# Another order in the opening of a state-space and feed-forward kernel: one chunk's C by heads, scores ahead of a mask difference, a held weight load, transposes behind the mixes

## The chip, the core and the metric

The kernel runs on one core of a Trainium2 chip. The metric is the device time in microseconds of one execution; the time before is the median of three runs. Engines are named as the profile names them: PE is TensorE, PEld its weight loads, DVE VectorE, ACT ScalarE, POOL GpSimd, SP SyncE. SP's and ACT's sequencers also issue the DMA transfers ("SPq", "ACTq" in the profile). All times inside an execution are counted from the start of the span.

## The reference

Two blocks in a row. The first is a state-space scan over 4 batches, 8 heads and 768 steps, with head width 32 and state width 16, in float32. In short:

```python
log_a = np.log(np.clip(a, 1e-06, 1.0))
for each chunk:                       # xc, Bc, Cc, la: the chunk's slices
    cum = np.cumsum(la, axis=-1)
    L = np.exp(cum[..., :, None] - cum[..., None, :]) * causal
    M = np.einsum('bhin,bhjn->bhij', Cc, Bc) * L
    y = np.einsum('bhij,bhjd->bhid', M, xc)
    y += np.einsum('bhin,bhnd->bhid', Cc, state) * np.exp(cum)[..., None]
    state = decay_full * state + sum over j of (Bc * xc * decay_from_j)
```

The second takes y as 3072 tokens of width 256: `h = y @ w_in` (256 x 2048), `g = h * clip(h + 3, 0, 6) / 6`, `out = g @ w_out` (2048 x 256). The two weight matrices are float64 in memory.

## The kernel before

The 768 steps are handled as six chunks of 128 (index `c`), each in two halves of 64 steps. For each chunk the kernel makes masks, scores, mixes and the new state, and from the chunk's y the feed-forward block `h`, `g` and `out`, which has most of the work. All instructions are written out in one order; every engine, and each queue of DMA issues, works through its own instructions in that order and waits by semaphores. Nothing is rescheduled. A wait thus holds up everything behind it on its engine. DMA semaphores are eight, shared in turn: a transfer that takes a semaphore again first waits until the transfer that had it before has landed.

The opening is the part up to the first `h` of chunk 0. Its steps, with the lines of the profile:

- ACT issues the first quarter of w_in (`load_w(0)`, L139, 1 MB into the tile `raw`) and then B (L94). SP issues `a` (L81), then chunk 0's C in eight transfers of 32 KB (`pairs_first`, L101, tile `pairs`: one for each batch and each parity of the head), then x (`load_x`, L119, tile `xt`), then the second quarter of w_in (`load_w(1)`, L139).
- From `a`, ACT and DVE make logarithms and running sums (L264, L266, L269), for the first two chunks first. PE turns these into differences in PSUM: a constant mask (L336, L343), then `diff`, which is `diff_less` (L348) and 16 small products `diff_pick` (L357) for each batch. ACT's exponentials make the decay tiles `L` of them (L365). Chunk 0's differences lie in banks f0 to f3, chunk 1's batches 0 and 1 in the banks "o", its batches 2 and 3 in the banks y0 and y1.
- PE transposes B (L422), ACT copies the result (L431, `bT`). DVE transposes C in squares (`turn_squares`, L465, `csT`) and makes two masked copies (`part_heads`, L475, `cT`). POOL fades half of csT (`fade`, L481) and scales B (`ends`, L396). DVE sums the remaining chunks' logarithms (`add_up`, L269) and SP stores them (`store_rows`, L286, L288).
- `busy` (L493) makes products with the identity whose result nobody reads: two ahead of the scores, one ahead of the mixes. Each is two MATMUL records of PE.
- `scores` (L530, tile `cb`) multiplies C and B into banks f0 to f3, and then `into_state` (L544) makes the parts of the new state in the banks y0 and y1. `multiply` has ACT copy these (L560, L569) and DVE multiply `L` by the scores in four instructions (L574).
- `turn_cum` (L316) transposes the running sums on PE into bank f1, and `by_token` (L319, DVE) stores them negated, for later chunks' masks.
- `mix` (L604) multiplies the masked scores and x, each half of the heads followed by the products with the mid-chunk state (`from_state`, L503). `keep` (L618, ACT) copies y for the feed-forward block.
- `renew` (L587, L554, DVE) makes the new state.

The float64 weights are decoded by hand, in five steps of a generator (`decode`; `weights(i, n)` runs n steps of part i): ACT extracts the top 16 bits (L198); DVE isolates exponent and sign (L215, L217) and makes the significand in two long operations (L201, L205); ACT builds the scale in two passes (L221, L223); DVE joins sign and scale (L228) and multiplies (L236) into `w_in` or `w_out`. Three `raw` buffers are used in turn.

After the opening, `mlp_in` (L626) makes `h` for 16 column blocks f of chunk 0 in the banks f0 to f3 in turn, each from two products that PE runs as four MATMUL records; ACT makes the ramp (L730) and DVE the product with it (L735, tile `gT`), which frees the bank. Block f uses weight part f // 4. The decoding of weight parts 2 to 5 is woven in between by f. Then come the output products `first_out` (L748), which need `gT` and the decoded `w_out`.

The order around the change is these lines of the kernel body:

```python
    turn_squares(bcs[0][0], turned(0)[2])      # L998
    part_heads(0)
    fade(0, HALF[1], nc.gpsimd)
    add_up(ends_at[1])
    store_rows()
    load_w(2)
    weights(0, 1)
    busy(2, ...)
    scores(0)
    multiply(0)
    load_w(3)
    turn_cum(c_ps)                             # L1010
    busy(1, ...)
    ...
    mix(0)                                     # L1015
```

Of the kernel before, what the change touches and what calls it, by code (L numbers as in the profile page):

```python
# [8 lines left out]
FP32 = mybir.dt.float32  # L9
# [12 lines left out]
def kernel(  # L22
# [24 lines left out]
    nc = tc.nc  # L47
    P = 128
# [37 lines left out]
    def load_bc(c):  # L86

        sl = slice(c * P, (c + 1) * P)  # L90

        def tokens_first(src, queue=nc.sync, **where):
            t = loads.tile([P, NB * NH, N], FP32, **where)
            queue.dma_start(out=t, in_=src[:, :, sl, :].rearrange("b h s n -> s (b h) n"))  # L94
            return t

        def pairs_first(src):
            t = loads.tile([P, 2, NB, 4, N], FP32, name="pairs", tag="bc")
            for b in range(NB):
                for h in range(2):  # L100
                    nc.sync.dma_start(  # L101
                        out=t[:, h, b].rearrange("s a n -> s (a n)"),
                        in_=src[b, h:NH:2, sl, :].rearrange("h (s a) n -> h s (a n)", a=4))
            return t

        if 0 < c < TURN:
            bcs[c] = [tokens_first(C, name="C", tag="bc")]
        Bs[c] = tokens_first(B, nc.scalar if c == 0 else nc.sync, name="B", bufs=1)
        if c == 0:
            bcs[c] = [pairs_first(C), Bs[c]]  # L110
        elif c < TURN:
            bcs[c].append(Bs[c])
        else:
            bcs[c] = [pairs_first(C), pairs_first(B)]
# [10 lines left out]
    NRAW = 3  # L125
    raws = {}

    def load_w(i, queue=nc.sync):

        raw = loads.tile([P, NK * FP * 2 * P], U32, name="raw", bufs=NRAW)  # L130
        if i < NP:
            cols = slice(2 * i * FP * P, 2 * (i + 1) * FP * P)
            src = moe_w_in[:, cols].rearrange("(k p) f -> p k f", p=P)
            dst = raw.rearrange("p (k f) -> p k f", k=NK)
        else:
            r0 = (i - NP) * FP * P
            src = moe_w_out[r0:r0 + FP * P, :].rearrange("(k p) m -> p k m", p=P)
            dst = raw.rearrange("p (k m) -> p k m", k=FP)
        queue.dma_start(out=dst, in_=src)  # L139
        raws[i] = raw  # L140
# [1 line left out]
    load_w(0, nc.scalar)  # L142
    load_bc(0)
    load_x(0)
    load_w(1)
    nc.scalar.preload_act_table_set("natural_log_exp_and_others")


# [38 lines left out]
    def decode(i):  # L187
# [20 lines left out]
            yield  # L208

        parts_m = significand()  # L210
        if i == 0:
            next(parts_m)
            next(parts_m)
        yield
# [70 lines left out]
    def store_rows():  # L285
        nc.sync.dma_start(  # L286
            out=cum_e[1:].rearrange("c g p -> g c p"), in_=cum_c[:, 1:])
        nc.sync.dma_start(  # L288
            out=cum_d[2:].rearrange("c a g i -> g (c a) i"),
            in_=cum[:, 2 * P:].rearrange("g (k i) -> g k i", i=HT))  # L290
# [178 lines left out]
    def part_heads(c):  # L469
        _, cT, csT = turned(c)  # L470
        for t in range(2):
            if c == TURN:
                nc.scalar.activation(cT[:, :, t], csT, AF.Copy, scale=parity[:, t:t + 1])
            else:
                nc.vector.tensor_scalar(  # L475
                    out=cT[:, :, t], in0=csT, scalar1=parity[:, t:t + 1], scalar2=None,
                    op0=ALU.mult)

    def fade(c, sl=slice(0, P), engine=nc.vector):
        csT = turned(c)[2][:, :, sl]  # L480
        engine.tensor_tensor(out=csT, in0=csT, in1=etos[c][:, :, sl], op=ALU.mult)  # L481
# [8 lines left out]
    def busy(n, bank):  # L490

        for _ in range(n):
            nc.tensor.matmul(  # L493
                out=bank.rearrange("p (b i) -> p b i", b=NB), lhsT=ident,
                rhs=ident.unsqueeze(1).to_broadcast([P, NB, P]), start=True, stop=True)
# [117 lines left out]
    def keep(c):  # L613

        yTs[c] = att.tile([P, NK, NB, P], FP32, name="yT", bufs=1)
        for a, u in ((0, 0), (0, 1), (1, 0), (1, 1)) if c else ((0, 0), (1, 0), (0, 1), (1, 1)):
            y, dst = ys[c][a, u], yTs[c][:, u, :, HALF[a]]
            nc.scalar.copy(out=dst, in_=y)  # L618
# [344 lines left out]
    def weights(i, n):  # L963
        for _ in range(n):
            next(parts[i], None)


    def diff(c, *bs):
        for part in (diff_less, diff_pick):
            for b in bs:  # L970
                part(c, b)
# [19 lines left out]
    for b in range(NB):  # L991
        ends(0, b)
    turn_b(0)
    diff(1, 0, 1)
    weights(0, 1)
    diff_exp(1, 2)
    diff_exp(1, 3)
    turn_squares(bcs[0][0], turned(0)[2])  # L998
    part_heads(0)
    fade(0, HALF[1], nc.gpsimd)  # L1000
    add_up(ends_at[1])
    store_rows()
    load_w(2)
    weights(0, 1)
    busy(2, ps.tile([P, NB * P], FP32, name="d", tag="f3"))
    scores(0)
    multiply(0)
    load_w(3)
    c_ps = ps.tile([P, NC, G], FP32, name="c_ps", tag="f1")
    turn_cum(c_ps)  # L1010
    busy(1, ps.tile([P, NB * P], FP32, name="d", tag="f0"))
    weights(0, 1)
    weights(1, 1)
    by_token(c_ps)
    mix(0)  # L1015
    keep(0)
    weights(1, 3)
    renew(0)
    weights(1, 1)
    load_eto(1)  # L1020
# [155 lines left out]
```

## Time and profile before

| what | value |
|---|---|
| time, median of 3 runs | 344.33 us (343.4 to 345.18) |
| profiled execution: its time | 343.4 us |
| profiled execution: its span | 341.7 us, granted clock 1.0 |
| PE busy | 333.8 us (98%) |
| DVE busy | 210.7 us (62%) |
| ACT busy | 188.3 us (55%) |
| POOL busy | 145.4 us (43%) |
| first score product (L530) | 15.20 us |
| first `h` product (L626) | 22.54 us |
| first output product (L748) | 50.11 us |

The span is the time from the first to the last instruction of the program; the execution's time has some 1.7 us more. The shares are averages over stages with different limits: in the opening PE waits for other engines and for DMA, from the first `h` product on it runs without a break. In lines of the chain of waits the numbers are the start, the length and what ran or was waited for; in lines of a timeline they are the start, the time from the first to the last of a merged group, the engine, the line, the operation, the tiles and, in brackets, the idle time before it with what ended it. The trace also holds a record of each DMA packet (queue, start, length, size) and of each increment of a DMA semaphore; from these come the times of packets and landings.

### The profile page before, as it was taken

The numbers are of one execution on the slowest core, as the hardware profiler recorded it, in microseconds if no ns is written. First come the engines' busy times: TensorE is split into PE (matmuls) and PEld (weight loads), VectorE is DVE, ScalarE is ACT, GpSimd is POOL, SyncE is SP. The second block draws the span as 40 slices with busy tenths as digits, with TensorE's granted clock in tenths as the row PEclk, the third lists the DMA queues.
The fourth block names the chain that finished last, engine by engine and source line by source line (L and its number), as shares of the span: only waits on it lengthen the run. The fifth ranks groups of instructions, "written<-read, shape, count | busy, mean of one in ns | idle before, by whom it ended". The sixth has DMA issues, their size and how long they took to land.

```text
span 341.7 us, 8203 instructions
## 1 busy us (share of the span) xinstructions
PE 333.8 (98%) x3372; PEld 267.5 (78%) x3372; DVE 210.7 (62%) x332; ACT 188.3 (55%) x394; POOL 145.4 (43%) x139
## 2 busy tenths in 40 slices
PE   5999999999999999999999999999999999999996
PEld 2554448888878888888888888888888888888996
DVE  6699999996499739665519465528465323465011
ACT  4778878667987481675471676470576030576000
POOL 3300000381282998099803089810089600079600
PEclk9999999999999999999999999999999999999999
DMA  8989967052690216167107294001260001110000
GB/s 172 174 312 197 209 233 153 2 59 69 164 114 8 58 55 119 25 84 70 24 27 144 33 96 62 16 2 18 33 75 2 2 4 17 30 17 2 0 33 31
DMA packets 89605, 25.15 MB, mean 74 GB/s; under 512 B 82208, under 2 KB 85952, under 8 KB 89056
## 3 DMA queue, kind: packets, MB, share of 16 engines
q1 hardware_dynamic: 85184, 23.33, 36.5%
q10 hardware_dynamic: 4384, 1.31, 1.8%
q8 instruction: 26, 0.43, 0.5%
q14 instruction: 11, 0.09, 0.1%
HBM read 21.33 MB, written 3.29 MB: 72 GB/s over the span
## 4 chain that ended last, share of the span: by engine, by line
PE 94%; DMA 3%; DVE 1%; SPq 1%; issue 0%; DVEq 0%
PE h L692 33%; PE wb L874 13%; PE wc L874 8%; PE o L748 8%; PE h L626 8%; PE wa L874 8%; PE oa L810 4%; PE ob L810 4%; PE y L604 3%; PE y L503 2%; PE cb L530 2%; DMA raw<-in_moe_w_in_dram 2%; PE y L544 1%; DMA pairs<-in_C_dram 1%; SPq L101 1%; DVE L L574 0%
## 5 line engine op out<-in xcount | busy, mean ns | idle before, releaser
L735 DVE SCALAR_TENSOR_TENSOR gT<-gT,h 128x512 f32<-128x512 f32 x96 | 64.9, 686 | 41.1 <-ACT gT L730 39.9
L730 ACT ACTIVATE gT<-h,half 128x512 f32<-128x512 f32 x96 | 65.2, 684 | 17.8 <-PE h L692 15.9
L796 POOL TENSOR_TENSOR s<-gT 128x512 f32<-128x512 f32 x20 | 28.9, 1443 | 76.2 <-DVE gT L735 76.1
L711 ACT ACTIVATE h<-h 128x512 f32<-128x512 f32 x62 | 35.8, 583 | 43.6 <-PE h L692 39.3
L692 PE MATMUL h<-y_hi,w_part 128*128 128x512 f32 x160 | 51.8, 409 | 0.0
L692 PE MATMUL h<-y_less,w_part 128*128 128x512 f32 x160 | 49.7, 397 | 0.0
L692 PE MATMUL h<-y_lo,w_part 128*128 128x512 f32 x160 | 49.5, 395 | 0.0
L692 PEld LDWEIGHTS h<-y_lo,w_part 128*128 128x128 f32 x160 | 30.0, 188 | 7.4
L692 PEld LDWEIGHTS h<-y_less,w_part 128*128 128x128 f32 x160 | 30.0, 188 | 6.9
L692 PEld LDWEIGHTS h<-y_hi,w_part 128*128 128x128 f32 x160 | 30.0, 188 | 6.8 <-DVE gT L735 0.4
L385 ACT ACTIVATE L<-L,cum_n 128x64 f32<-128x64 f32 x128 | 31.6, 338 | 0.0
L874 PE MATMUL wb<-s,w_out 128*128 128x256 f32 x128 | 30.6, 382 | 0.0
L748 PE MATMUL o<-w_out,gT 128*128 128x256 f32 x128 | 28.8, 381 | 0.0
L626 PE MATMUL h<-yT,w_in 128*128 128x512 f32 x64 | 27.7, 594 | 0.0
L748 PEld LDWEIGHTS o<-w_out,gT 128*128 128x128 f32 x128 | 24.1, 190 | 3.8 <-issue 0.5
L403 POOL TENSOR_TENSOR tmp<-state,eto 128x256 f32<-128x256 f32 x5 | 3.4, 673 | 55.3 <-ACT eto L389 55.2
L874 PEld LDWEIGHTS wb<-s,w_out 128*128 128x128 f32 x128 | 24.0, 190 | 3.6
L796 POOL TENSOR_TENSOR s<-gT,s 128x512 f32<-128x512 f32 x20 | 26.0, 1306 | 1.3
L796 POOL TENSOR_TENSOR gT<-gT 128x512 f32<-128x512 f32 x20 | 25.7, 1291 | 1.3
L796 POOL TENSOR_TENSOR s<-s,gT 128x512 f32<-128x512 f32 x20 | 25.7, 1290 | 0.0
L158 POOL TENSOR_SCALAR_AFFINE_SELECT L<-L 64x1024 f32<-64x1024 f32 (+1 forms) x16 | 20.4, 1280 | 10.5 <-DMA L<-cum_d 10.1
L396 POOL TENSOR_TENSOR bs<-B,L 128x128 f32<-128x128 f32 x24 | 12.7, 545 | 26.0 <-ACT L L385 20.9
(138 smaller groups left out, 507.5 us busy)
## 6 DMA issues: line engine op xcount, KB each, us to landing
raw<-in_moe_w_out_dram SPq DMA_DIRECT2D x4, 1024.0 KB
L<-cum_d SPq DMA_DIRECT2D x8, 512.0 KB
xt<-in_x_dram SPq DMA_DIRECT2D x6, 512.0 KB
raw<-in_moe_w_in_dram SPq DMA_DIRECT2D x3, 1024.0 KB
out_dram<-back SPq DMA_DIRECT2D x128, 16.0 KB
pairs<-in_C_dram SPq DMA_DIRECT2D x40, 32.0 KB
eto<-cum_e SPq DMA_DIRECT2D x20, 64.0 KB
B<-in_B_dram SPq DMA_DIRECT2D x5, 256.0 KB
```

The source lines that it names most:

```text
L158: nc.gpsimd.affine_select(out=t[rows], in_=t[rows], pattern=pattern, compare_op=ALU.is_ge, fill=-1e5, base=base, channel_multiplier=-1)
L385: nc.scalar.activation(Ls[c][:, b, h], Ls[c][:, b, h], AF.Exp, bias=cum_n[:, c, g:g + 1])
L396: nc.gpsimd.tensor_tensor(out=bss[c][:, hs], in0=Bs[c][:, hs], in1=Ls[c][:, b, :, HT - 1:HT].to_broadcast([P, NH, N]), op=ALU.mult)
L626: nc.tensor.matmul(out=h, lhsT=w_in[f // FP][:, j, f % FP * P:(f % FP + 1) * P], rhs=yTs[k][:, j].rearrange("p b i -> p (b i)"), start=(j ...
L692: nc.tensor.matmul(out=hs_[k, f], lhsT=w[j][:, f % FP * P:(f % FP + 1) * P], rhs=y[:, j], start=(start and j == 0), stop=True, skip_group_ ...
L711: nc.scalar.activation(h, h, AF.Copy, scale=1.0 / EPS + 1.0)
L730: nc.scalar.activation(gTs[k][:, f], h, AF.Relu, bias=half, scale=1.0 / 6.0)
L735: nc.vector.scalar_tensor_tensor(out=g, in0=g, scalar=1.0, in1=h, op0=ALU.min, op1=ALU.mult)
L748: nc.tensor.matmul(out=o[:, b % 2], lhsT=gTs[0][:, f, b * P:(b + 1) * P], rhs=w_out[:, f], start=(f == 0 and b % 2 == 0), stop=True, skip_ ...
L796: nc.gpsimd.tensor_tensor(out=o, in0=p_, in1=q_, op=op)
L810: nc.tensor.matmul(out=bank[:, slot], lhsT=lhs[:, j], rhs=rhs[:, j], start=(clear and j == 0), stop=True, skip_group_check=True)
L874: nc.tensor.matmul(out=bank[:, slot], lhsT=lhs[:, j], rhs=rhs[:, j], start=(clear and j == 0), stop=True, skip_group_check=True)
```

## The change

Six things, all in the opening. Chunk 0's C is loaded by `heads_first`: again eight transfers of 32 KB into the same places of the same tile, but one for each head, over 32 partitions and all four batches. Batch 1's difference of chunk 1 goes from ahead of the scores to behind `scores(0)`. The second quarter of w_in is no longer issued behind x, but behind `part_heads(0)`: DVE writes one column of its buffer, and the load waits for that. The first two decode parts, no longer only the first, do their two long DVE operations ahead of the exponent's. `turn_cum` stands behind `mix(0)` and takes bank f2, not f1, and `by_token` stands behind `keep(0)`. The three idle products are gone. Lines of the kernel behind L139 have numbers higher by 10 or so in the changed file; the texts use those of the kernel before.

```diff
+        def heads_first(src):
+            t = loads.tile([P, 2, NB, 4, N], FP32, name="pairs", tag="bc")
+            for h in range(NH):
+                rows = slice(32 * (h // 2), 32 * (h // 2) + 32)
+                nc.sync.dma_start(
+                    out=t[rows, h % 2].rearrange("s b a n -> s b (a n)"),
+                    in_=src[:, h, sl, :].rearrange("b (s a) n -> s b (a n)", a=4))
+            return t
...
-            bcs[c] = [pairs_first(C), Bs[c]]
+            bcs[c] = [heads_first(C), Bs[c]]
...
-    def load_w(i, queue=nc.sync):
+    def load_w(i, queue=nc.sync, held=False):
         raw = loads.tile([P, NK * FP * 2 * P], U32, name="raw", bufs=NRAW)
+        if held:
+            nc.vector.memset(raw[:, 0:1], 0)
...
     load_x(0)
-    load_w(1)
...
-        if i == 0:
+        if i < 2:
             next(parts_m)
             next(parts_m)
...
-    diff(1, 0, 1)
+    diff(1, 0)
     weights(0, 1)
...
     part_heads(0)
+    load_w(1, held=True)
     fade(0, HALF[1], nc.gpsimd)
     add_up(ends_at[1])
     store_rows()
+    weights(0, 1)
+    scores(0)
+    diff(1, 1)
+    multiply(0)
     load_w(2)
+    load_w(3)
     weights(0, 1)
-    busy(2, ps.tile([P, NB * P], FP32, name="d", tag="f3"))
-    scores(0)
-    multiply(0)
-    load_w(3)
-    c_ps = ps.tile([P, NC, G], FP32, name="c_ps", tag="f1")
+    mix(0)
+    c_ps = ps.tile([P, NC, G], FP32, name="c_ps", tag="f2")
     turn_cum(c_ps)
-    busy(1, ps.tile([P, NB * P], FP32, name="d", tag="f0"))
-    weights(0, 1)
-    weights(1, 1)
+    keep(0)
     by_token(c_ps)
-    mix(0)
-    keep(0)
-    weights(1, 3)
+    weights(1, 4)
     renew(0)
     weights(1, 1)
```

## The prediction

> **What bounds the kernel.** I read the busy shares first: PE 98% of a span of 341.7 us, clock 10 tenths in every slice. Then the chain that ended last, in order of time: PE carries it without a gap from 22.5 us to the end, so a change in the opening is worth what it moves the first `h` product (L626) and lets the stages behind it follow. The opening is this part of the chain (start, length, what; us):
>
> ```profile
> 8.82 3.97 DMA pairs<-in_C_dram
> ...
> 12.97 1.18 DVE csT L465
> ...
> 14.17 0.89 DVE cT L475 x2
> ...
> 15.20 1.25 PE cb L530 x59
> ...
> 16.45 1.30 DVE L L574 x2
> ...
> 17.79 0.43 PE c_ps L316 x4
> 18.22 1.05 PE d L493 x2
> 19.28 0.85 PE y L604 x51
> 20.13 0.17 issue
> ...
> 22.61 27.66 PE h L626 x64
> ```
>
> The reader is to see four things: C's last transfer lands at 12.79; the masks and scores follow it; the sums' transposes and one idle product stand between scores and mixes; and the mixes stop once for "issue", a wait for nothing that the profile shows.
>
> Third, DVE's timeline, because its share of the slices from 25 to 60 us is 9 tenths or more. It runs nearly without gaps from the first weight multiply to the first output weights:
>
> ```profile
> 25.30 0.69 DVE L228 TENSOR_TENSOR we<-we,ws 128x1024 uint16<-128x1024 uint16 x1 [0.65 <-ACT we L223]
> ...
> 27.16 1.28 DVE L735 SCALAR_TENSOR_TENSOR gT<-gT,h 128x512 f32<-128x512 f32 x2
> ...
> 48.13 1.23 DVE L236 SCALAR_TENSOR_TENSOR w_out<-wm,we 128x1024 f32<-128x1024 f32 x1
> ```
>
> PE starts the output products (L748) at 50.11, and the multiply that they need ends at 49.36. **Slack 0.75.** The fourth quarter of w_in has 0.77 (42.35 against 12 x 1.7155 behind 22.54). From L735 at 27.16 the DVE and ACT orders are those of the changed kernel too, with no wait for PE on DVE, so the stretch 27.16 to 49.36 is taken as rigid (22.2): **the end moves by the move of the first gT, less up to 0.75.** This is the frame of every sum below.
>
> Last, the DMA queues, for the "issue":
>
> ```profile
> q8 instruction: 26, 0.43, 0.5%
> ```
>
> 26 packets, 16384 bytes each: PE's code. For PE's 6775 records that is some 63 bytes each; I take 64, so 256 instructions a packet. In the packet records the second starts at 17.85, takes 1.01, and the stop ends at 20.29, 2.44 behind that start. Counting PE's records, the stop stands before number 705, and 705 is 3 x 256 less 63. I read it as PE emptying a queue of some 64 while its fourth packet of code is not there yet. In stages with little traffic a packet starts when PE is some 100 instructions ahead of a multiple of 256, plus 1.05 us (1.0 to 1.1 in six of them). By that the packet of 17.85 was asked for at 15.9 and due at 16.95. What lay between is the first `raw` load on SP's queue (weights 1): its 4096-byte packets ran 14.53 to 18.2. The next code packet was due at 20.8 and started at 24.29; raw 2's last increment is at 24.26. The third started at 31.56; raw 4's last increment is 31.58. **Code waits for the weight load on its DMA engine.** [...]
>
> **Part by part.**
>
> *C by heads.* Eight transfers of 32 KB before and after. Before, each C semaphore rises in one first write and four single steps, x's in sixteen: four engines against sixteen, and C's 256-byte packets run from 5.79 to 11.7. Issues unhindered take 0.56 to 0.62; the sixth still waits for weights 0 (landing 6.67), as its semaphore is shared. Sixth to eighth now stand at 6.70, 7.35, 8.0. First packets come 1.03 (a) to 1.55 (x) behind an issue, landings 0.35 (B) to 1.35 (C) behind the last packet: 9.5 to 11.0, value 10.6, in the middle, since no row has this form. If sixteen engines aren't used it stays 12.79. DVE is free at 10.2: csT 10.75, cT done 2.08 later (12.97 to 15.05), 12.85, scores 12.95 to 14.2.
>
> *Scores behind, one difference moved.* Chunk 1's batch 1 difference (0.217 + 0.09 + 16 x 0.0196 + switch, 0.7) moves behind the state products. The state products (L544) can't use this whole gain: their banks hold chunk 1's other differences until ACT's two exponentials (L365, 13.31 to 14.39) end, and nothing of that moves. So 14.45, not 14.05. x lands 5.35 (first engine) to 6.1 behind its issue, now 8.65: 14.0 to 14.75, value at most 14.45, since B and C no longer hold four engines back. State products 0.75, difference 0.7: first mix at 15.9. DVE: scan to 14.05, four L574 of 0.6 from 14.2; the mixes' second half needs the fourth at 16.7. That hides.
>
> *No idle products.* Two of three (1.98) lay in the wait for cT: nothing. The third, 1.05, was on the path, as the chain shows: gone. What PE's clock makes of it is a rival.
>
> *Transposes behind the mixes.* 0.43 leaves the path ahead of the mixes and comes back behind them, 0.36. The cost is on DVE: the negated sums (L319) wait for PE there, with all weight decoding queued behind. Before, 20.72. And decode 1 now puts its two long operations first, so ACT's two passes start later. From L319 to the first gT it took 6.44 with 0.65 idle; now 0.20 + 0.72 + 1.14 + 0.42 (exponent) + 0.05 + 1.15 + 0.03 + 1.15 (ACT) + 0.04 + 0.72 + 1.14 = 6.76.
>
> *Weights 1 held.* One memset (0.06) on DVE, and SP's load waits for it: 12.75 to 13.25 instead of 10.43. Behind it on SP stand the sums' stores, which wait for the scan at 14.05 anyway, then weights 2 and 3. x used the engines until 15.1 before and until some 13.9 now, so the load starts 13.9 to 14.5 (1.1 to 1.3 behind issue), value 14.1, and on the engine of the code ends 3.3 later (14.53 to 17.85), **17.4**. ACT reads it at 19 or later: hidden as data.
>
> **The sum.** PE's numbering loses 12 records ahead of the mixes for the idle products; 8 for the transposes. Record 412, where the third refill is asked for, is now among the state products, 14.5; due 15.55, inside the weight load; starts 17.4; usable 2.44 later, **19.85**. Record 705 is now 7 records into the first inter-chunk products (L503), which PE reaches at 15.9 + 0.8 = 16.7. PE stands 3.15. Then 0.5 (rest of L503), 0.79 (L604), 0.61 (L503): transposes at 21.75, first `h` 22.1 (before 22.54), sums at DVE 22.2, first gT 28.95, 1.8 later than 27.16. Less 0.7 of slack: **+1.1**. The profiled execution is 343.4 (span 341.7 and 1.7 around it): 344.5. The median of the runs shown is 0.93 above it: **345.4**. With the load's end 0.6 either way, 344.8 to 346.0.
>
> **Rivals.**
>
> 1. *Code is there in time.* For: only one stop of 0.38 shows it, and what happens between a packet's end (18.86) and 20.29 isn't shown. Then mixes 15.9 to 18.7, transposes, `h` 19.06, sums 19.17, gT 25.93: 1.23 earlier, plus slack: -1.9, 342.4. Against: three packets that start at a load's end. Chance 0.18.
> 2. *Code late, but let in between.* Due 15.55, usable 18.0, stop 1.3: gT 27.2, level with before; only the slack is won: -0.65, 343.7. Chance 0.13.
> 3. *The clock falls* (the other side). PE stands 3.15 at one place, and no product fills it. Before, its longest stand was 1.68 (5.80 to 7.48), harmless: the products behind took 0.217. The start shows the price: 0.427 for eight of L336, until 5.5. If the stop lasts long enough, the 1.9 of small products behind it cost up to 1.9 more, value 1.0, and the first 3.4 of `h` take twice that; the latter lies half in DVE's 0.75: total +2.6, 346.9. It decides from the stop's length, which no row places between 1.68 and 3.15. [...] Chance 0.09.
> 4. *C doesn't come sooner.* Everything from cT on stands as before, the held load starts at 16.4, code 19.7, usable 22.1: +3.4, 347.7. Against: the four steps. Chance 0.04.
>
> **Chances.** The forecast 0.56; 0.18, 0.13, 0.09, 0.04 for the rivals. The bound of 0.5% is 1.72 us, about what a measurement of this kernel tells from no change. The forecast passes it on the slow side one time in six (0.09), rival 3 nearly always, rival 4 always: slower 0.21. Rival 1 passes it six times in ten, and little else: faster 0.12. Within: 0.67. Range: 342.4 keeps half of rival 1; 346.8 keeps the forecast's slow tail and part of rival 3.
>
> **What would show it.** C's last landing near 10.6 and cT at 12.85; state products at 14.45 behind ACT's L365; weights 1's first packet near 14.1; the second code packet near 17.4; a stop of PE named "issue" of about 3 in L503 ahead of the second mixes; L319 at 22.2, first gT at 28.95, L748 at 51.2. Wrong if PE passes from mixes to `h` without the stop (L626 at 19.1), if the stop is shorter than 1.5, or if `h` or the mixes run at twice their length.

## The result, and the profile after

The changed kernel takes 348.8 us (median of 4, 347.87 to 350.53), the kernel before 343.99 beside it on the same chip (median of 4, 343.4 to 345.18): ratio 1.0141, 95% interval 1.0092 to 1.019. It is slower, by 4.8 us where 1.1 was forecast, and outside the range. The profiled execution took 348.97 with a span of 347.3.

The lines of the changed file behind L139 have numbers higher by 10: L636 is `h`, L513 the products with the state, L614 the mixes, L554 the state products, L329 the negated sums, L745 the first `gT`, L758 the output products. In the files of the experiments the shift is 0 to 13.

The clock's row of the changed kernel's page, which was 9 in all slices before:

```profile
PEclk9967999999999999999999999999999999999999
```

The trace's clock records give the stretches: half clock from 15.90 to 19.31 and from 22.73 to 29.55, full otherwise from 5.66, where the records begin, to 346.99. The records of the kernel before show full clock from 5.66 to 343.6.

The chain that ended last, in the opening (start, length, what ran or was waited for):

```profile
7.42 4.12 DMA pairs<-in_C_dram
...
12.86 0.88 DVE cT L485 x2
...
13.89 1.20 PE cb L540 x61
...
15.44 0.75 issue
...
19.60 3.21 issue
...
23.82 1.11 PE y L614 x61
24.93 1.04 PE y L513 x16
25.97 0.56 PE c_ps L326 x4
26.53 29.18 PE h L636 x64
55.72 4.50 PE o L758 x20
```

Four things are to be seen. C lands at 11.54, 1.25 sooner than before, and the scores start at 13.89 instead of 15.20. Then PE stops twice for "issue": 0.75 among the state products, which the prediction does not have, and 3.21 in the first L513, the place that was forecast. And what follows the second stop runs at half clock: L513 takes 1.04 for sixteen where 0.61 was forecast, L614 1.11 where it was 0.79, `h` 29.18 where it was 27.66.

VectorE's timeline shows what waits for the end of this chain (start, time, line, operation; in brackets the idle time before and what ended it):

```profile
18.27 1.23 DVE L246 SCALAR_TENSOR_TENSOR w_in<-wm,we 128x1024 f32<-128x1024 f32 x1
26.57 0.29 DVE L329 TENSOR_SCALAR cum_n<-c_ps 128x128 f32<-128x128 f32 x1 [7.08 <-PE c_ps L326]
...
33.33 1.28 DVE L745 SCALAR_TENSOR_TENSOR gT<-gT,h 128x512 f32<-128x512 f32 x2
```

In the kernel before, the negated sums did not wait:

```profile
20.72 0.28 DVE L319 TENSOR_SCALAR cum_n<-c_ps 128x128 f32<-128x128 f32 x1
```

The first gT is at 33.33, 6.17 behind the kernel before; the output products at 55.66 on PE's timeline, 5.55 behind; the profiled execution 5.57 behind. So the frame held in its numbers: the move of the first gT less some slack is the move of the end. It is not the only path there, though. PE runs the `h` products from 26.46 to 55.66 without a wait, and the `w_out` multiply ends at 55.51: either would have set the output products within 0.15. What remains is why the first gT is 4.4 later than forecast.

### The profile page after: what moved, and what is told of

It is laid out like the page before. It is cut to its first block, busy times and chain, and to the rows that moved or that the text cites. A ratio compares the mean times of both kernels' runs of the same rounds, so it can differ in the third digit from the quotient of the medians.

```text
span 347.3 us, 8195 instructions
## 1 busy us (share of the span) xinstructions
PE 335.1 (96%) x3366; PEld 268.7 (77%) x3366; DVE 213.3 (61%) x333; ACT 187.5 (54%) x394; POOL 146.0 (42%) x139
## 4 chain that ended last, share of the span: by engine, by line
PE 94%; DMA 3%; issue 1%; DVE 1%; SPq 0%; DVEq 0%
PE h L702 32%; PE wb L884 12%; PE h L636 8%; PE wc L884 8%; PE o L758 8%; PE wa L884 8%; PE oa L820 4%; PE ob L820 4%; PE y L614 3%; PE y L513 2%; PE cb L540 2%; DMA raw<-in_moe_w_in_dram 2%; PE y L554 2%; DMA pairs<-in_C_dram 1%; DVE csT L475 0%
## 5 line engine op out<-in xcount | busy, mean ns | idle before, releaser
L745 DVE SCALAR_TENSOR_TENSOR gT<-gT,h 128x512 f32<-128x512 f32 x96 | 64.9, 685 | 41.2 <-ACT gT L740 39.9
L636 PE MATMUL h<-yT,w_in 128*128 128x512 f32 x64 | 29.3, 619 | 0.0
L758 PE MATMUL o<-w_out,gT 128*128 128x256 f32 x128 | 28.9, 381 | 0.0
L758 PEld LDWEIGHTS o<-w_out,gT 128*128 128x128 f32 x128 | 24.0, 190 | 4.1 <-ACT gT L740 0.7
L168 POOL TENSOR_SCALAR_AFFINE_SELECT L<-L 64x1024 f32<-64x1024 f32 (+1 forms) x16 | 21.2, 1331 | 9.8 <-DMA L<-cum_d 9.4
L636 PEld LDWEIGHTS h<-yT,w_in 128*128 128x128 f32 x64 | 12.7, 201 | 15.8 <-issue 14.0
```

Of the source, the lines that this page charges most:

```text
L168: nc.gpsimd.affine_select(out=t[rows], in_=t[rows], pattern=pattern, compare_op=ALU.is_ge, fill=-1e5, base=base, channel_multiplier=-1)
L636: nc.tensor.matmul(out=h, lhsT=w_in[f // FP][:, j, f % FP * P:(f % FP + 1) * P], rhs=yTs[k][:, j].rearrange("p b i -> p (b i)"), start=(j ...
L745: nc.vector.scalar_tensor_tensor(out=g, in0=g, scalar=1.0, in1=h, op0=ALU.min, op1=ALU.mult)
L758: nc.tensor.matmul(out=o[:, b % 2], lhsT=gTs[0][:, f, b * P:(b + 1) * P], rhs=w_out[:, f], start=(f == 0 and b % 2 == 0), stop=True, skip_ ...
```

## The experiments

Three theories stood against each other. **A, code:** PE's instructions come in packets of 16384 bytes; the packet wanted at record 705 (start 20.45 in the changed kernel, 17.85 before) waits for loads, and the stop sets the end. **B, idle products:** without them the clock falls, and that is the cost. **C, the sums:** VectorE's wait for the transposes (7.08) is the cost. Each kernel was timed in five rounds beside the kernel before, whose medians were 344.1 to 344.3.

This table collects what the texts below use. PE's records, weight loads included, are counted from 0. The packet starts come from the packet records; the stop is the gap ahead of record 705, from the end of the records before it to its start (the 0.38 of the kernel before, in the prediction and in the expectations, runs from start to start); half clock comes from the clock records up to 35 us (one window is 3.41; in e13 and e15 one window of it lies early, at 8.2 to 11.7). All but the ratio is from one profiled execution of each kernel.

| kernel | ratio to before (95%) | 1st / 2nd code packet | stop at 705 | half clock | first gT |
|---|---|---|---|---|---|
| before | 1 | 10.69 / 17.85 | 0.17 | 0 | 27.16 |
| changed | 1.0141 (1.0092 to 1.019) | 13.51 / 20.45 | 3.21 | 10.2 | 33.33 |
| e1_idle | 1.0167 (1.0147 to 1.0186) | 13.61 / 19.57 | 3.20 | 6.8 | 32.06 |
| e2_unheld | 1.0133 (1.0113 to 1.0152) | 13.45 / 18.53 | 2.52 | 6.8 | 31.16 |
| e3_later | 1.0074 (1.0058 to 1.009) | 13.59 / 17.69 | 0 | 3.4 | 29.89 |
| e4_heads | 1.0111 (1.0082 to 1.014) | 13.46 / 19.59 | 2.17 | 3.4 | 29.21 |
| e5_heads_x | 1.011 (1.0078 to 1.0143) | 10.68 / 19.33 | 1.87 | 3.4 | 28.45 |
| e6_pairs | 1.0168 (1.0144 to 1.0193) | 10.90 / 20.39 | 3.72 | 10.2 | 33.31 |
| e7_noidle | 1.0093 (1.0067 to 1.0119) | 10.65 / 18.49 | 0.68 | 13.7 | 28.66 |
| e8_sums | 1.0069 (1.0044 to 1.0093) | 10.56 / 18.13 | 1.19 | 0 | 29.80 |
| e9_second_late | 0.9992 (0.9976 to 1.0008) | 10.89 / 18.20 | 0.56 | 0 | 27.37 |
| e10_sums_ahead | 1.0129 (1.0107 to 1.0152) | 13.42 / 19.23 | 2.88 | 10.2 | 29.52 |
| e11_combo | 1.0087 (1.0061 to 1.0112) | 11.06 / 18.06 | 2.86 | 6.8 | 28.62 |
| e12_between | 1.0158 (1.0125 to 1.0191) | 10.90 / 16.92 | 1.19 | 6.8 | 30.77 |
| e13_between2 | 1.0094 (1.0064 to 1.0124) | 13.74 / 17.70 | 1.05 | 6.8 | 29.22 |
| e14_heads_w2 | 0.999 (0.9973 to 1.0007) | 12.85 / 17.17 | 0 | 0 | 26.45 |
| e15_after_w2 | 1.0079 (1.0061 to 1.0098) | 13.59 / 18.38 | 1.97 | 10.2 | 30.72 |

### The two idle products ahead of the scores put back

```diff
     weights(0, 1)
+    busy(2, ps.tile([P, NB * P], FP32, name="d", tag="f3"))
     scores(0)
```

> The changed kernel with one edit: the two idle products that the kernel before has ahead of the scores are put back there. They take 1.98 at full clock and start at 12.35, so the scores start at about 14.35 where the changed kernel has 13.89. Theory A (the end is set by the stop for code, 3.21 at record 705, and by the halved clock behind it, 22.73 to 29.55, which that stop brings; the first halving, 15.90 to 19.31, only shortens the stop in front of it): the clock stays full from 15.90 to 19.31, the state products and first mixes take 1.2 to 1.5 less, PE comes to record 705 earlier or at the same time and stands there as long or longer, the second halving stays, and the time is that of the changed kernel within 0.5 us. Theory B (the missing idle products are what costs: with them the clock stays full all the way): both halvings go, the first gT comes 2 to 3 us earlier and the time falls by 2 to 4 us.

349.56 us, no better than the changed kernel. The first half-clock window is gone, as A said, and PE comes to record 705 1.0 sooner, at 18.61; it stands there 3.20 and the second stretch of half clock follows, 22.69 to 29.52. **These two buy nothing while the stop is there.** B alone does not explain the changed kernel.

### The weights' load not held

```diff
     load_x(0)
+    load_w(1)
...
-    load_w(1, held=True)
```

> The changed kernel with the second weights' load unheld, behind x's load as in the kernel before. Theory A (code waits for the weight load's packets): the load's packets run right behind x's and the first code packet, from about 13.5 to 18, instead of 14.5 to 20; the second code packet starts near 18 instead of 20.45, the stop at record 705 falls from 3.21 to about 1, the window 19.31 to 22.73 is mostly worked, and the second halving of the clock goes or shrinks: 2 to 4 us faster than the changed kernel. Rival (the hold is harmless or helps C and x; what costs is the order of the sums' transposes and the missing idle products): the stop stays near 3, or C and x land later by 0.5 and more, and the time stays within 1 us of the changed kernel.

348.44. The code packet starts at 18.53, near the 18 that A gave, and the stop shrinks, but to 2.52 and not to 1: PE, too, came to it 1.0 sooner, at 18.63, since the state products kept the full clock. The time stays, as the rival had it. The hold as such costs or gains next to nothing here.

### The weights' load held longer

```diff
-    load_w(1, held=True)
...
     multiply(0)
+    load_w(1, held=True)
     load_w(2)
```

> The changed kernel with the hold of the second weights' load put later on VectorE: behind the four decay multiplies of chunk 0 (to about 17.5) instead of behind the masks (12.9). The load is then issued near 17.9 and its first packet comes near 19. Theory A (the second code packet waits for nothing but this load): it is asked for near 16.2 and starts near 17.3, is usable near 19.7, the stop at record 705 shrinks to less than 1, the clock's second halving goes, the first h product starts near 22.5 to 23.5 instead of 26.5; the load lands near 23.5, which may hold ScalarE's copy of its upper halves by up to 1: the time falls by 3 to 5 us, to the kernel before or within 1.5 of it. Rival (the stop has another cause than the queue, such as the latency of a code packet or PE's own order): the stop stays at 2 to 3 and the time changes by under 1 us; or the weights are now late and give back all of it.

346.78, 2.0 off. The packet starts at 17.69 ahead of the weights, and the 3.21 are gone, as these lines of PE's timeline show:

```profile
19.61 0.92 PE L513 MATMUL y<-csT,mid 32*64 32x64 f32 x16
...
22.23 7.13 PE L636 MATMUL h<-yT,w_in 128*128 128x512 f32 x16
30.63 3.70 PE L636 MATMUL h<-yT,w_in 128*128 128x512 f32 x8 [1.27 <-DVE gT L745]
```

The first products with the state, and so record 705, run through, and `h` starts 4.2 sooner (22.23 against 26.46). So what PE waits for there hangs on that load: nothing else was moved, and the packet starts 2.76 sooner. But the gain of 4.2 on PE is not had: `h` then waits 1.27 for DVE. The chain of this kernel names the new bound:

```profile
17.92 5.39 DMA raw<-in_moe_w_in_dram
...
24.06 1.23 DVE wm L215
...
26.84 1.16 ACT we L233
...
29.89 1.28 DVE gT L745 x2
```

The weights land at 23.3, and their five decoding steps stand between that and the first gT. **A load late enough to let the code pass is here too late for its data.** That was expected to cost up to 1; it costs the part of the gain that is missing.

### C by heads alone

```diff
-            bcs[c] = [pairs_first(C), Bs[c]]
+            bcs[c] = [heads_first(C), Bs[c]]
```

> The kernel before with the loads of C by heads alone. C's last increment is expected at 11.5 as in the changed kernel, 1.25 earlier than 12.79. Theory A: cT is there near 13.8, but the two idle products hold PE until 14.7, so the scores start 0.5 earlier (14.7 against 15.20); the second code packet waits for the second weights' load as before (start 17.85 or 0.3 sooner), so the stop in front of record 705 grows by what the scores gain, from 0.38 to 0.6 to 0.9, and the time is that of the kernel before within 0.5 us. Rival (C's earlier landing is worth its 1.2 us or the 0.5 of the scores): the first gT comes earlier by as much, 0.5 to 1.2 us off the time.

347.69: this one part costs 3.4 us by itself, against both expectations. C does land earlier and the scores start 0.3 earlier (14.87), but the second code packet starts at 19.59 instead of 17.85. The first one is late too, 13.46 instead of 10.69. The packet records show x's 128-byte packets from 9.7 on, where the kernel before has them from 11.0: the eight issues take SyncE 6.95 instead of 8.16, so x is issued at 8.25 instead of 9.47 and gets ahead of the first code packet. The next run asks whether that lateness is what is handed on.

### C by heads, with x's issue where it was

```diff
-    load_x(0)
-    load_w(1)
...
     weights(0, 1)
+    load_x(0, held=True)     # a memset on VectorE at 9.5
+    load_w(1)
```

> The kernel before with C by heads, and x's load held back on SyncE by a memset that VectorE reaches at about 9.5, where SyncE issued x before (9.47); with C by heads alone it was issued at 8.25, its packets began at 9.6, ahead of the first code packet, which started at 13.46 instead of 10.69, and the second one at 19.59 instead of 17.85. Theory A (C by heads frees SyncE sooner, x's packets get ahead of the first code packet, and that lateness is handed on to the second): the first code packet is back at 10.5 to 11, the second at 17.5 to 18.2, the stop at record 705 falls from 2.17 to 1 or less, the clock stays full, and the time goes from 347.7 to 343.5 to 344.5. Rival (C's own packets on all sixteen engines, or the clock alone, make C by heads slow): the first code packet stays behind 12.5 and the time above 346.5.

347.97. The first packet is back at 10.68, and nothing else changes: the second starts at 19.33. My mended theory fell; lateness is not handed on from packet to packet. SyncE's timelines of this kernel (first fence) and of the kernel before (second) show what else had moved:

```profile
14.54 0.41 SPq L295 DMA_DIRECT2D cum_e<-pre  x1
15.00 0.43 SPq L297 DMA_DIRECT2D cum_d<-pre  x1
15.47 1.38 SPq L150 DMA_DIRECT2D raw<-in_moe_w_in_dram  x2
```

```profile
16.20 0.34 SPq L286 DMA_DIRECT2D cum_e<-pre  x1
16.59 0.44 SPq L288 DMA_DIRECT2D cum_d<-pre  x1
17.07 2.19 SPq L139 DMA_DIRECT2D raw<-in_moe_w_in_dram  x2
```

The two stores of the sums wait for DVE's scan, the scan for C. With C sooner, the stores and the third weights behind them are issued 1.6 sooner. By the prediction's estimate PE asks for the second packet at record 412, which it reaches at 15.39 here and at 15.84 in the kernel before. So the stores now stand ahead of that request and the third weights beside it, where both stood behind it. That is tested further down (e9, e14, e15).

### The change without C by heads

```diff
-            bcs[c] = [heads_first(C), Bs[c]]
+            bcs[c] = [pairs_first(C), Bs[c]]
```

> The changed kernel with C loaded in pairs as in the kernel before; all else of the change is kept. Theory A: SyncE issues x at 9.5 again, the first code packet is back at 10.7 and the stop of 0.75 at record 449 goes; but C lands at 12.8, so cT is there at 15.05, the held load is issued near 15.1, just when record 412 asks for the second code packet; that packet goes ahead of the weights (start near 16.5 to 17.5, stop 1 or less, time 345 to 346.5) or falls behind them (start near 20.5, stop over 3, time 349 to 350). PE also stands 2.5 ahead of the scores with no idle products, so one window at half clock is expected either way. Rival (the order of the sums and the missing idle products are what costs, the loads nothing): the time stays at the changed kernel's 348.8 within 0.5 with no stop longer than 1.

350.29, the second branch of A: first packet at 10.9, second behind the held weights at 20.39, stop 3.72. It is no faster than the changed kernel (ratios 1.0168 and 1.0141, with intervals that overlap), so within the change C by heads is not what costs.

### No idle products, nothing else

```diff
-    busy(2, ps.tile([P, NB * P], FP32, name="d", tag="f3"))
     scores(0)
...
-    busy(1, ps.tile([P, NB * P], FP32, name="d", tag="f0"))
```

> The kernel before without its three idle products, nothing else changed. Theory A: the two ahead of the scores lay in the wait for cT; the third held the mixes for 1.05, so PE reaches record 705 sooner, but the second code packet still starts at 17.85 and is usable at 20.29: the stop grows from 0.38 to about 1.4 and no time is won there. Theory on the clock: the wait of 2.4 from 12.7 to 15.1 brings one window at half clock behind it (the state products to the first mixes, 15.9 to 19.3), which costs up to 1.2 ahead of the stop and is then hidden by it: the time is that of the kernel before within 0.5. Rival (without the idle products the clock falls for two windows and into the h products, as in the changed kernel): 2 to 4 us slower.

347.74, 3.5 slower: here the rival was right. The page's clock row and the chain of this kernel:

```profile
PEclk9957999999999999999999999999999999999999
```

```profile
21.95 1.11 PE y L604 x61
...
24.11 5.90 PE h L626 x7
```

The clock is at half from 15.85 to 29.51, four windows in a row. Behind the wait for cT (2.03 without a product, from 13.14) the small products take longer (sixteen L503 1.05 where the kernel before has 0.61, L604 1.11 where it has 0.79) and `h` starts at 24.0 instead of 22.5. PE also stands 0.68 ahead of record 705. The profile puts part of this down to ACT's first y copy, but record 705 starts at 20.73, ahead of that copy's increment at 20.79, and 2.24 behind the start of the packet, as in the other kernels: this too is a stop for code. **With the idle products the clock of this kernel stays full, without them it is at half for 13.7, and their absence costs 3.5.**

### The sums' transposes behind the mixes, nothing else

```diff
-    c_ps = ps.tile([P, NC, G], FP32, name="c_ps", tag="f1")
-    turn_cum(c_ps)
     busy(1, ...)
     weights(0, 1)
-    weights(1, 1)
-    by_token(c_ps)
     mix(0)
+    c_ps = ps.tile([P, NC, G], FP32, name="c_ps", tag="f2")
+    turn_cum(c_ps)
     keep(0)
-    weights(1, 3)
+    by_token(c_ps)
+    weights(1, 4)
```

and the first two decode parts with their long operations first, as in the change.

> The kernel before with the row sums' transposes, their negation and the second weights' long VectorE passes in the order of the changed kernel, nothing else changed. Theory A: the transposes leave the path ahead of the mixes (0.43), but the stop at record 705 is fixed by its code packet at 20.29, so PE ends the mixes at the same time, 22.1, and does the transposes to 22.5; VectorE stands from 20.7 to 22.5 for them with the decoding behind it; the first gT comes at 29.2 instead of 27.16 and the time rises by 1.2 to 1.9 us. Rival (VectorE's wait is hidden, as VectorE has slack): within 0.5 us of the kernel before.

346.84, 2.6 slower, with the clock at full all the way. The stop is 1.19, VectorE stands 2.30 for the transposes (its L319 is at 23.04), the first gT is at 29.80. The sum was made for 1.2 to 1.9. The stop is longer, since the mixes start sooner, but it ends at 20.34, as in the kernel before (20.30). What the sum had wrong is the end of the mixes: 22.1, where it is 22.64 here and 22.61 in the kernel before; that 0.5 is most of the rest. So C is a cost of its own in the kernel before.

### C by heads, with the stores and the third weights held back

```diff
-    store_rows()
-    load_w(2)
...
     multiply(0)
+    load_w(2, held=True)     # a memset behind the four decay multiplies
+    store_rows()
```

on top of C by heads and x held to 9.5.

> The kernel before with C by heads and x held to 9.5 (as in the run of that name), and in addition the third weights' load (weights 2) held by a memset behind VectorE's four decay multiplies, with the two stores of the row sums behind it on SyncE. Theory A, as mended by the last runs: the second code packet goes behind all that SyncE has issued before the packet is asked for (near 16). With C earlier the scan, and so the stores (15.0, 15.1) and weights 2 (15.5, 15.9), were issued 1.1 to 1.5 sooner than in the kernel before (16.2, 17.1) and got ahead of it. Held back, the packet follows weights 1's own packets: start 18.1 to 18.6 instead of 19.3, usable near 20.5 to 21, stop at record 705 0.8 to 1.3 instead of 1.87, clock full, time 345 to 346.5 against 347.97. Rival (only weights 1 matters, the stores and weights 2 nothing): start 19.3 again, stop 1.9, time 347.5 to 348.5.

343.78 against 344.2: the 3.8 us that the kernel without the hold loses (e5) are gone, more than expected. The chain of this kernel:

```profile
19.94 0.56 issue
...
22.82 27.66 PE h L637 x64
```

The packet starts at 18.20, 0.15 ahead of the first of the second weights' sixteen landings (18.35 to 19.04), and not at 19.33; the stop is 0.56 and no window of half clock follows. **The packet had been waiting for the stores and the third weights too.** The two were not held one at a time. In e3 only the stores ran ahead of the packet, and it started 2.42 behind record 412; with neither ahead of it that was 2.11 (e12) and 1.64 (e13). So the stores alone look small, but this compares single traces.

### The sums put back ahead of the mixes, the rest of the change kept

The second decode part's passes are put back in their old order too.

```diff
-    mix(0)
-    c_ps = ps.tile([P, NC, G], FP32, name="c_ps", tag="f2")
+    c_ps = ps.tile([P, NC, G], FP32, name="c_ps", tag="f1")
     turn_cum(c_ps)
-    keep(0)
+    weights(1, 1)
     by_token(c_ps)
-    weights(1, 4)
+    mix(0)
+    keep(0)
+    weights(1, 3)
```

> The changed kernel with the row sums' transposes, their negation and the order of the second weights' VectorE passes put back to where the kernel before has them (ahead of the mixes); the rest of the change is kept. Theory A: the stop at record 705 and the clock's halving stay (stop 3.0 to 3.5, end near 22.8), but VectorE no longer stands 7.08 for the transposes; it does the second weights' passes during the stop, ScalarE's two passes follow the last y copy at 26.3, and the first gT comes at 30.5 to 31.2 instead of 33.33: 2.1 to 2.8 us off, 346.0 to 346.7. Rival (the transposes' place costs nothing, since the h products are late anyway): 348.8 within 0.5.

348.76: no gain. VectorE does the second weights' passes during the stop and the first gT is at 29.52, 3.8 sooner than in the changed kernel. Yet PE is as late: `h` starts at 24.97 and takes 30.42 behind the stop and at half clock (20.24 to 30.48), and the output products start at 55.23 against 55.66. The line of `h` in its chain:

```profile
24.97 30.42 PE h L636 x64
```

**Two chains are late together, and taking away one shows nothing.** In this state of the kernel C is not the bound, and "the first gT sets the end" is no longer true: with the clock down, PE is.

### Three attempts to beat both

The first takes the kernel with the stores held and has one idle product ahead of the scores and none ahead of the mixes:

```diff
-    busy(2, ps.tile([P, NB * P], FP32, name="d", tag="f3"))
+    busy(1, ps.tile([P, NB * P], FP32, name="d", tag="f3"))
...
-    busy(1, ps.tile([P, NB * P], FP32, name="d", tag="f0"))
```

> An attempt to beat both: the run with weights 2 and the stores held, with one idle product ahead of the scores instead of two and none ahead of the mixes. The scores start near 13.9 (cT) instead of 14.8, the mixes some 1.9 earlier than there; the second code packet is asked for about 1 sooner, near 15.2, but still waits for weights 1's packets (18.1 to 18.6): the stop grows to 2.5 to 3.2. Theory A: the end is set by that packet, and the long stop brings a half-clock window behind it: 346 to 348, no better than that run. Rival (the earlier scores and the shorter idle work carry through): 343 to 344.5.

347.14, as A said: PE is 2.4 earlier at record 705 and stands 2.86 for the same packet (18.06), and the clock is at half for 6.8. **Two idle products, 1 to 2 us of PE's time ahead of a stop, cost nothing here: they fill it.**

The second also holds the second weights, between the code's request and its due time, and has their long VectorE passes first:

```diff
         if c == 0 and q == 0:          # behind the first decay multiply
+            load_w(1, held=True)
```

> The same attempt with weights 1 held as well, behind the first decay multiply (near 15.9, issue near 16, first packet near 17), and with its long VectorE passes ahead of its short ones. Theory A: the second code packet, asked for near 15.2 to 15.5, finds only x's packets (to 15.2) and starts at 16.3 to 16.8, ahead of weights 1; it is usable near 19, PE comes to record 705 at about 17.7, the stop is 1.0 to 1.5 and the clock stays full or has one window of half. Weights 1 land near 21.5, which puts the first gT at 27.5 to 28.8: 344 to 346, the best version with C by heads. Rival (something else than the loads delays the packet): start after 18, stop over 2.5, 347 or more.

349.21. The packet did what A said (16.92, stop 1.19), but the order I had written put the negated sums behind the weights' passes, and PE's second mixes need the sums' bank, as the chain shows:

```profile
16.16 5.62 DMA raw<-in_moe_w_in_dram
...
23.75 0.21 DVE cum_n L330
...
24.01 1.16 PE y L617 x60
```

PE stood 3.62 for a bank. The third attempt mends that:

```diff
-    weights(1, 1)
     by_token(c_ps)
+    weights(1, 1)
     mix(0)
```

> The last kernel of the attempts (weights 1 held behind the first decay multiply) with the negation of the row sums put ahead of the second weights' VectorE passes, so that TensorE's second mixes, whose bank the sums hold, no longer wait for weights 1 (3.62 at record 746). Theory A: the second code packet starts near 16.9 again, the stop at record 705 is about 1.2 and ends near 19.3, the clock stays full, TensorE ends the mixes near 21.3. Weights 1 land at 21.8 again; VectorE's passes and ScalarE's two follow, the first gT comes at 28.5 to 29 (27.16 in the kernel before): 345 to 346, so that a code packet ahead of the weights is paid for by later weights. Rival (what counts is TensorE alone): 343 or less, faster than both.

346.97. The stop is 1.05, but the weights land at 22.65, the first gT is at 29.22. In the profiled execution a half-clock window also fell into 8.2 to 11.6, so that the scores started 1.25 later than in the run before (15.41 against 14.16); so up to about that much of it may not be the load's. The direction is A's: a packet ahead of the weights is paid for with later weights.

### C by heads, x early, the stores and the third weights held

```diff
-    store_rows()
-    load_w(2)
...
     multiply(0)
+    load_w(2, held=True)
+    store_rows()
```

on top of C by heads alone.

> The kernel before with C by heads, x as early as that makes it (8.3), and weights 2 and the stores held behind the decay multiplies. The first code packet is late again (13.4 to 13.6). Theory A: with the idle products in place TensorE reaches record 449 near 16.5, when that packet is just usable (2.4 to 2.7 behind its start), so its lateness costs 0 to 0.3 by itself; the second packet starts behind weights 1's packets on its queue, 17.5 to 18.7: stop 0.3 to 1.2 at record 705, time 343.5 to 345. Rival (the lateness of the first packet is handed on to the second and to the end): start 19 or later, 346.5 to 348.

343.58 against 344.06, the lowest of all, though the interval of the ratio (0.9973 to 1.0007) does not tell it from the kernel before. The first packet is late (12.85) and it hardly matters: with the idle products in place PE ends what stands ahead of record 449 at 15.82 and goes on at 16.03. The second starts at 17.17, and there is no stop at all in the chain:

```profile
18.68 1.12 PE y L615 x57
...
21.30 0.61 PE y L514 x16
21.91 27.66 PE h L637 x64
```

### The changed kernel, with the stores and the third weights held

```diff
-    store_rows()
     weights(0, 1)
     scores(0)
     diff(1, 1)
     multiply(0)
-    load_w(2)
+    load_w(2, held=True)
+    store_rows()
```

> The changed kernel with one thing altered: weights 2 held by a memset behind VectorE's four decay multiplies, the two stores of the sums behind it on SyncE. Theory A: the second code packet no longer has the stores and the first packets of weights 2 ahead of it; it starts right behind weights 1's own packets, 18.6 to 19.2 instead of 20.45; usable near 21 to 21.6, stop 1.7 to 2.3 instead of 3.21; the half clock behind it falls from two windows to one or stays: 1 to 2.5 us off, 346.3 to 347.8. The rest, up to the 344.2 of the kernel before, is then weights 1 alone (held to 13.8) and the clock. Rival (weights 2 and the stores are not ahead of it): start 20.4 again and 348.8 within 0.5.

346.98, 1.8 off. The packet starts at 18.38 instead of 20.45, the stop is 1.97, and half clock from 21.96 to 28.79 remains, as the chain shows:

```profile
18.84 1.97 issue
...
23.93 30.10 PE h L636 x64
```

So of the changed kernel's late packet up to 2.1 are the stores and the third weights. It may be less: in e1 and e10, whose loads have the changed kernel's order, the packet starts at 19.57 and 19.23, and these are single traces. The 2.9 that are left to the kernel before I put down to the second weights' own load, the sums and the clock; no run takes all of these away at once from the changed kernel.

## Why the prediction was wrong, point by point

**The frame held, in part by luck.** From the first gT to the output products it took 22.3 (22.25 in the forecast), and from VectorE's L329 to the first gT 6.76, the figure of the sum to the hundredth. But the sum has no path over PE alone, and PE alone was as late: in e10 the first gT comes 3.8 sooner and the output products only 0.43. Wrong were two terms ahead of it; they make 4.37, all of the difference at L329 (26.57 against 22.2).

**The term that was mis-sized: the code packet.** "On the engine of the code ends 3.3 later, 17.4" failed; it started at 20.45, 3.05 later. The reading behind it, that the packet waits for loads, held where only loads and stores were moved (17.69 in e3, 18.38 in e15); that they share one DMA engine is an estimate of mine from the times, since the packet records name a queue and no engine. Right, too, was the time from its start to record 705: 2.4 in the forecast, 2.2 to 2.6 in the fifteen kernels that stop there, whatever instruction the record is. But I followed only the second weights. I wrote of the sums' stores that they "wait for the scan at 14.05 anyway", and did not go on: the scan was sooner than before by C's gain, so the stores and the third weights were issued 1.3 sooner and passed the packet. Holding these alone moves it to 18.38 (e15). The remaining 1.0 is the late start of the second weights: C landed at 11.54 and not at 10.6, so their load was issued at 13.80 and not near 13.0, with the first packet at 14.83 where 14.1 was forecast (15.24 in e15, 3.14 ahead of the code packet; the forecast allowed 3.3).

**A stop I did not look for.** SyncE issues x 1.46 sooner, and the first code packet falls behind x: 0.75 at record 449. I had listed this earlier issue as a gain for x only. With the idle products in place an equally late packet costs little (e14). In the changed kernel the end of the second stop hangs on the second packet, so the 0.75 should come off that stop's length and not add to the end; no run shows this by itself.

**The stop's length was right by luck.** 3.15 forecast, 3.21 found: the packet was 3.05 late, and PE was 2.9 late as well (19.60 against 16.7), from C (0.9), the first stop (0.75) and the first half-clock window.

**The other side was underrated.** Rival 3 is what happened beside the forecast. Its price was 1.0 for the small products, up to 1.9; the trace gives 3.76 from the stop's end to L329, against 2.35 in the sum: 1.4. The 3.4 of `h` at twice the time in the rival's sum had no row behind it; what the changed kernel shows is half clock from 22.73 to 29.55, two steps of 3.41, of which `h` had the last 3.0, and `h` took 29.18 where it took 27.66. "No row places" the length from which it decides between 1.68 and 3.15; the stop of 1.87 (e5) already had a window behind it, those of 1.19 and 0.56 (e8, e9) did not. The chance of 0.09 was an estimate, and far too small. The trace's windows are 3.41 long, and none with half clock behind it was empty: in the changed kernel PE stood for 3.13 of the 3.41 ahead of 22.73, and 2.03 without a product, with small products around, were enough in e7.

**"Two of three lay in the wait: nothing"** was wrong in the same way. Alone, their removal costs 3.5 (e7). In the changed kernel putting two of the three back gains nothing (e1): the stop stays, and half clock follows it all the same.

**"C sooner" as a gain** was wrong as a part. Alone it costs 3.4 (e4); with the stores and the third weights held back it costs nothing and gains nothing that can be measured (e9, e14).

**The costs do not add.** C by heads 3.4, no idle products 3.5, the sums 2.6: 9.5 by themselves, 4.8 together. As I read it, all three end in one place, between record 705 and the first `h` or the first gT behind it, and there they overlap.

So the faster case was rightly held small, and the slower one, at 0.21, was far too small: I priced one mechanism with care and gave its neighbours single chances, although each of them leads into the same stop.

## What to carry to other kernels

When an edit frees a queue or ends a wait, list everything that is issued sooner because of it, down to small stores, and ask what it now overtakes; here the victim was the engine's own code, which no line of the kernel issues. In a stage of many short matmuls, count instructions as well as time: some 250 of them took less time than the next packet with a bulk load in front of it (in the kernel before 3.8 us from record 449 to 705, and 4.5 from record 412, where by the estimate the packet is asked for, to the end of the stop). Do not take out filler for being filler: ask first which wait it lies in and what the clock does without it.

## What the runs showed of the hardware

- PE's code: 26 packets of 16384 bytes per execution. In the opening all stops for it stood exactly ahead of records 449 and 705 (256 apart). At record 705 PE went on 2.2 to 2.6 us behind the start of the packet; at record 449, where it stood over 0.5, 2.7 to 3.0 behind it. There was no stop at record 705 in two kernels of the seventeen (e3, e14); the longest was 3.72 (e6).
- The packet's turn: in the changed kernel it came behind the second weights, the two stores and 161 of the third weights' 256 packets. Holding the stores and the third weights back moved its start by 1.13 (e9, 19.33 to 18.20) and 2.07 (e15, 20.45 to 18.38). By what rule it is served is not settled.
- The clock: its records change only at steps of 3.41 us counted from the first one (in the changed kernel at 15.90, 19.31, 22.73 and 29.55). Once down, it stayed down for one to four windows (3.4 to 13.7 us). It was longest in e7 (13.7 us), where short matmuls on parts of the array filled most of the time up to 24.0; PE stood for 0.2 and 0.7 of the first two of these four windows, and for nothing of the third.
